# Attention and routed experts on one core: probabilities times values of a head pair in one block per pair where there were two

## The chip, the cores and the metric

The kernel runs on one NeuronCore of one Trainium2 chip. The metric is the device time of one execution in microseconds (us). Lower is better.

## The reference

Causal attention with a bias from running sums, over 8 batches, 8 heads, 576 positions and a head size of 64, in fp32. Its output, reshaped to 4608 tokens of 512 features, goes through a layer of eight experts of which each token uses one.

```python
scores = scale * np.matmul(q, k.transpose(0, 1, 3, 2))
cum = np.cumsum(np.maximum(s, 0.0), axis=-1)
bias = -(cum[:, :, :, None] - cum[:, :, None, :])
scores = np.where(causal, -1000000000.0, scores + np.minimum(bias, 0.0))
attn = np.exp(scores - np.max(scores, axis=-1, keepdims=True))
attn = attn / (np.sum(attn, axis=-1, keepdims=True) + 1e-09)
x = np.matmul(attn, v)                    # -> (4608, 512)
logits = x @ w_gate + modality_bias[modality_id]
e_idx = np.argmax(logits, axis=1)         # one expert for each token
out[mask] = gate_w[mask, None] * (np.maximum(x[mask] @ w1[e], 0.0) @ w2[e])
```

## The kernel before

The first stage is attention. It goes through 32 pairs: a pair is one head of two batches, called `ab` = 0 and 1. The queries of a pair are cut into nine tiles: tiles 0 to 3 are the four blocks of 128 queries of `ab` = 0, tiles 4 to 7 those of `ab` = 1, and tile 8 holds the last 64 queries of both. Tile c (or 4 + c) sees 128 (c + 1) keys because of the mask. `ORDER` takes them as 3, 7, 2, 6, 8, 1, 5, 0, 4.

For each tile there are two steps.

- `score`: TensorE multiplies queries by keys (lines 373 and 395, for tile 8 lines 408 and 409) into a PSUM buffer `sp`, of which there are four (`SPB`). VectorE adds the mask and finds the row's bound (line 397, for tile 8 line 411), and ScalarE takes the exponential and the row's sum (line 417, a column of `sums`).
- `trans`, which I call the turn of a tile: TensorE transposes the exponentials, 128 keys at a time (line 427; line 440 for tile 8), into a PSUM buffer `pt`, of which there are two, and ScalarE copies them into `PT` (line 430; for tile 8 VectorE does, line 446). In a row, the number of transposes or the width tells the tile: four of them (512 columns) are tile 3 or 7, three tile 2 or 6, two tile 1 or 5, one tile 0 or 4. So a copy of 128 columns on line 430 is that of tile 0 or of tile 4.

The turn of a tile is written down three tiles behind its score (`LAG`), so the turns of a pair reach into the scores of the next one. There are three `PT` tiles, and a pair uses two of them.

`tail` is the last step of a pair: the turned probabilities times the values (line 467). The result has the head's 64 features on 64 partitions, and the two batches of a pair stand on partitions 0 to 63 and 64 to 127 of one PSUM tile `o`; each of these matmuls uses one half of TensorE's columns. Keys are summed over five blocks j of 128. Before the change there are two such blocks of matmuls for each pair. Block `g` = 1 covers queries 256 to 575. It is written down after the turn of tile 8, and has ten matmuls. Block `g` = 0 covers queries 0 to 255. It is written down after the turn of tile 4, the last one, and has four. An fp32 matmul shows as two records in the trace, two passes over its columns, so the blocks are 20 and 8 records there.

After a block ScalarE copies 256 columns of `o` into `oT` (line 470), VectorE copies the last 64 queries (line 474), ScalarE adds a small number to the sums (`rs`, line 479), VectorE inverts them (line 480), TensorE multiplies `oT` by a unit matrix with the gate's weights beside it (`pw_`, line 347) into the PSUM tile `ox`, and VectorE scales that by `rs` into `x` (lines 489 and 491).

GpSimd prepares the next pair's queries and keys (lines 323 and 327). The core's order on each engine is made by the scheduler of the framework from the order of the program text and from explicit "issue after" edges; each engine then works through its own list in order.

The second stage is the experts. Its first instruction on TensorE is line 1032 (`tp`), and then lines 1082 and 1057 follow.

Of the kernel before, what the change touches and what calls it, by code (L numbers as in the profile page):

```python
# [7 lines left out]
F32 = mybir.dt.float32  # L8
# [3 lines left out]
AF = mybir.ActivationFunctionType  # L12
ALU = mybir.AluOpType
# [4 lines left out]
P = 128  # L18
KW = 576
XW = 72  # L20

PTS, PTW = 448, 1984
NEG = -8.0e9
EXT = 76
ORDER = (3, 7, 2, 6, 8, 1, 5, 0, 4)
LAG = 3
TD = 1
SPB = 4
# [9 lines left out]
class Attn:  # L38
# [406 lines left out]
                        w = PT[ab][:kp, PTW - 64:].unsqueeze(1)  # L445
                    cp(w, pt[:kp, :P * nj].rearrange("p (j a q) -> p a j q", a=2, q=64)[:, ab])  # L446

    def tail(self, st, g):

        nc = self.nc  # L450
        V, PT, x, h = st["V"], st["PT"], st["x"], st["h"]
        for _ in range(TD):
            yield
        q0, q1 = (256, KW) if g else (0, 256)
        o = st["o"] if g else self.ps2.tile([P, 512], F32, name="o")
        oT = self.oT[st["pi"] % 2]

        pe, self.pe = self.pe, []
        nj = 5 if g else 2
        for j in range(nj):  # L460
            f = max(P * j, q0)
            for ab in range(2):
                r = slice(64 * ab, 64 * ab + 64)
                with ExitStack() as after:
                    for i in pe:
                        after.enter_context(self.tc.issue_after(i))
                    m = nc.tensor.matmul(o[r, f - q0:q1 - q0], V[:, ab, j, :], PT[ab][:, PTS * j + f if j < 4 else PTW - 64:PTS * j + q1 if j < 4 else PTW], start=j == 0, stop=j == nj - 1)  # L467
            pe = [m.ins]
        self.wall = m.ins
        nc.scalar.copy(oT[:, q0:q0 + 256], o[:, :256])  # L470
        if g:
            for ab in range(2):
                r = slice(64 * ab, 64 * ab + 64)
                nc.vector.tensor_copy(oT[r, 512 + 64 * ab:576 + 64 * ab], o[r, 256:320])
        yield
        n = 5 if g else 4
        rs = self.sm.tile([P, 5], F32, name="rs")
        with self.tc.issue_after(self.hold[0]), self.tc.issue_after(self.act):
            nc.scalar.activation(rs[:, :n], st["sums"][:, 4 * g:4 * g + n], AF.Identity, bias=self.eps[:, :1])
            nc.vector.reciprocal(rs[:, :n], rs[:, :n])  # L480
        xo = self.xo
        for u in range(2):
            c = 2 * g + u
            self.pw_(xo[:, 2 * XW * u:2 * XW * u + 2 * XW], oT[:, P * c:P * c + P], self.pw[:, h, :], start=True, stop=True)
        if g:
            self.pw_(xo[:, 4 * XW:5 * XW], oT[:, 512:], self.pq[:, h, :], start=True, stop=True)
        src = xo[:, :4 * XW].rearrange("p (t d) -> p t d", t=4)
        rv = rs[:, :4].unsqueeze(2).broadcast_to([P, 4, XW])
        nc.vector.tensor_tensor(x[g][:, :, :, h], src.rearrange("p t (d r) -> p t d r", r=2), rv.rearrange("p t (d r) -> p t d r", r=2), ALU.mult)
        if g:  # L490
            nc.vector.tensor_scalar(x[2][:, 0, :, h], xo[:, 4 * XW:5 * XW].rearrange("p (d r) -> p d r", r=2), rs[:, 4:5], None, ALU.mult)
        yield

    def run(self, npair, newx, done, setup):

        bg = self.bg = []
        seq = [(pi, i) for pi in range(npair) for i in ORDER]
        sts = {}
        prev, prepg, n = [], None, len(seq)
        for k in range(n + LAG + 9):  # L500
            if k < n:
                pi, i = seq[k]
                if k % 9 == 0:
                    sts[pi] = self.start(pi, newx(pi // 8) if pi % 8 == 0 else sts[pi - 1]["x"])
                    prepg = self.prep(pi + 1) if pi + 1 < npair else None
                with self.behind() if pi or not self.pe else self.tc.issue_after(self.pe[-1]):
                    self.score(sts[pi], i)
                if k in setup:
                    with self.newest():
                        more = setup[k]()  # L510
                        if more is not None:
                            bg.append([more, False])
                if k % 9 == 2 and 0 < pi < npair - 1:
                    self.V[pi + 1] = self.load_v(pi + 1)
                if k % 9 == 7 and 0 < pi < npair - 2:
                    self.raw[pi + 2] = self.load_qk(pi + 2)
                if prepg is not None:
                    next(prepg, 0)
            if prev and next(prev[0][0], 0) == 0:
                _, st, g = prev.pop(0)  # L520
                if g == 0 and st["pi"] % 8 == 7:
                    bg.append([done(st["pi"] // 8, st["x"]), False])
            for j in () if k == LAG else (0, 1) if k == LAG + 1 else (k - LAG,) if LAG < k < n + LAG else ():
                p0, i0 = seq[j]
                with self.behind():
                    self.trans(sts[p0], i0)
                if i0 in (8, ORDER[-1]):
                    g = int(i0 == 8)
                    prev.append((self.tail(sts[p0], g), sts[p0], g))
            if not prev and k >= n + LAG:  # L530
                break
            for b in list(bg):
                if k >= b[1] if b[1] > 1 else k % 9 in QUIET or not b[1]:
                    with self.newest():
                        b[1] = next(b[0], None)
                    if b[1] is None:
                        bg.remove(b)
        assert not prev
        return bg
# [847 lines left out]
```

## Time and profile before

| | |
|---|---|
| median of three runs | 836.78 us (836.66 to 837.16) |
| the profiled execution, its own time | 836.83 us |
| its span, first to last instruction | 835.1 us |
| mean granted TensorE clock | 0.995 |
| busy share of the span: PE, DVE, ACT, POOL | 98%, 65%, 65%, 43% |
| line 467 runs, from its first to its last start | 22.9 to 384.8 us |
| the experts' first matmul on TensorE (line 1032) | 386.17 us |

PE is TensorE's matmuls, PEld its weight loads, DVE is VectorE, ACT is ScalarE, POOL is GpSimd and SP the queue that issues transfers. "Busy" is the time that an engine spent on instructions. Matmuls are pipelined, so the record of a matmul is longer than the distance to the next one, and it is the distance from start to start that tells what it costs.

### The profile page before, as it was taken

To read this page: it belongs to the slowest core of one execution; us is meant where nothing else is said; L and a number is where in the kernel's file an instruction comes from. 1 tells how busy PE (TensorE), PEld (TensorE's weight loads), DVE (VectorE), ACT (ScalarE), POOL (GpSimd) and SP (SyncE) were. 2 spreads that over 40 slices of the span, in tenths; PEclk is the share of its full clock that TensorE was granted. 3 is DMA by queue.
4 is the path that set the end of the run, shared out by engine and by line. 5 is a ranking of instruction groups with operands and counts; after the bars stand their busy time and mean duration, and the time that the engine had idled before them with its cause. 6 is when DMAs were issued, how large, how long until landed. Compare 5 with 4: busy or idle time off the path is not lost. (4 is left out here: it accounts for less than half of the span.)

```text
span 835.1 us, 16829 instructions
## 1 busy us (share of the span) xinstructions
PE 818.3 (98%) x5692; PEld 715.2 (86%) x5692; DVE 545.9 (65%) x1502; ACT 542.1 (65%) x1292; POOL 359.9 (43%) x384
## 2 busy tenths in 40 slices
PE   7999999999999999999999999999999999999996
PEld 7888888888888888887888999998888999988884
DVE  7666667667666677666579865556666655655874
ACT  6788888888888888786365554444555554444763
POOL 8959768887698867993500100000000000000010
PEclk9999999999999999999999999999999999999998
DMA  7665556676557656547498776555556666555960
GB/s 235 180 198 180 178 190 196 213 230 190 167 178 222 196 177 193 175 164 279 173 397 316 297 273 246 205 207 199 214 207 252 255 256 225 216 207 209 376 231 29
DMA packets 68549, 182.31 MB, mean 218 GB/s; under 512 B 7993, under 2 KB 8889, under 8 KB 68334
## 3 DMA queue, kind: packets, MB, share of 16 engines
q1 hardware_dynamic: 62622, 161.17, 57.0%
q0 software_dynamic: 5840, 20.06, 6.2%
q8 instruction: 45, 0.74, 0.4%
q14 instruction: 42, 0.34, 0.1%
HBM read 144.73 MB, written 26.80 MB: 205 GB/s over the span
## 5 line engine op out<-in xcount | busy, mean ns | idle before, releaser
L1068 POOL DMA_INDIRECT out<-ys,oi x36 | 36.5, 1015 | 368.4 <-ACT ys L1067 299.9
L397 DVE CUSTOM_DVE_ANT_0 pe<-sp,mk 128x512 f32<-128x512 f32 (+3 forms) x256 | 120.7, 488 | 57.7 <-PE sp L395 55.2
L417 ACT ACTIVATE pe<-pe,mx 128x512 f32<-128x512 f32 (+3 forms) x256 | 144.5, 565 | 15.6 <-DVE mx L397 10.2
L430 ACT COPY PT<-pt 128x512 f32<-128x512 f32 (+3 forms) x256 | 106.7, 417 | 31.0 <-PE pt L427 27.8
L427 PE MATMUL pt<-ident,pe 128*128 128x128 f32 x640 | 119.2, 284 | 0.7 <-ACT PT L430 0.2
L467 PE MATMUL o<-PT,V 128*64 128x320 f32 (+4 forms) x896 | 108.8, 364 | 2.7 <-DVE PT L446 2.6
L467 PEld LDWEIGHTS o<-PT,V 128*64 128x64 f32 x896 | 75.1, 136 | 36.2 <-DVE PT L446 8.8
L1084 ACT ACTIVATE hT<-hp 128x512 fp32r<-128x512 f32 x72 | 42.8, 595 | 93.1 <-PE hp L1082 92.6
L373 PE MATMUL sp<-KA,QH 128*128 128x256 f32 (+2 forms) x256 | 100.2, 398 | 2.5 <-POOL KA L236 1.8
L427 PEld LDWEIGHTS pt<-ident,pe 128*128 128x128 f32 x640 | 76.2, 144 | 16.1 <-ACT PT L430 6.1
L1082 PE MATMUL hp<-xT,wcb 128*128 128x256 f32 x648 | 89.6, 282 | 0.0
L1082 PE MATMUL hp<-xT,wca 128*128 128x256 f32 x624 | 87.3, 282 | 0.5 <-ACT xT L1034 0.5
L327 POOL TENSOR_TENSOR KA<-rawk,KA 64x576 fp32r<-64x576 f32 x62 | 87.3, 1426 | 0.2
L395 PE MATMUL sp<-KB,QL 76*128 76x256 f32 (+2 forms) x256 | 86.1, 338 | 1.0 <-DMA QL<-ek 1.0
L327 POOL TENSOR_TENSOR QL<-rawq,QH 64x576 fp32r<-64x576 f32 x62 | 86.6, 1413 | 0.2
L1085 DVE SCALAR_TENSOR_TENSOR hT<-hp,hT 128x512 fp32r<-128x512 f32 x72 | 49.5, 688 | 54.7 <-ACT hT L1084 54.5
L1082 PEld LDWEIGHTS hp<-xT,wcb 128*128 128x128 f32 x648 | 83.1, 188 | 0.6
L1082 PEld LDWEIGHTS hp<-xT,wca 128*128 128x128 f32 x624 | 80.4, 188 | 1.4 <-issue 0.7
L1057 PE MATMUL y<-wcb,hT 128*128 128x512 f32 x336 | 81.2, 398 | 0.0
L1057 PEld LDWEIGHTS y<-wcb,hT 128*128 128x128 f32 x336 | 62.8, 188 | 14.7
L323 POOL TENSOR_SCALAR KA<-rawk 128x576 fp32r<-128x576 f32 x60 | 39.4, 670 | 60.2 <-PE sp L373 43.8
L1082 PE MATMUL hp<-xT,wcc 128*128 128x256 f32 x456 | 64.6, 281 | 0.0
(285 smaller groups left out, 1638.4 us busy)
## 6 DMA issues: line engine op xcount, KB each, us to landing
wrbw<-in_w SPq DMA_DIRECT2D x104, 512.0 KB
wraw<-in_w SPq DMA_DIRECT2D x56, 512.0 KB
rawq<-in_qkv SPq DMA_DIRECT2D x31, 576.0 KB
rawk<-in_qkv SPq DMA_DIRECT2D x31, 576.0 KB
xg<-lists SPq DMA_DIRECT2D x18, 576.0 KB
V<-in_qkv SPq DMA_DIRECT2D x32, 320.0 KB
KB<-KA SPq DMA_DIRECT2D x62, 144.0 KB
lists<-z SPq DMA_DIRECT2D x8, 576.0 KB
```

What stands on the lines that cost most here:

```text
L327: self.last = nc.gpsimd.tensor_tensor(o, i, h, ALU.subtract).ins
L373: self.pe.append(self.nc.tensor.matmul(sp[:, :nn], QH[:, q0:q0 + P], self.KA[u][:, ab, :nn], start=True, stop=False).ins)
L395: self.pe.append(nc.tensor.matmul(sp[:, :nn], QL[:EXT, q0:q0 + P], KB[:EXT, ab, :nn], start=False, stop=True).ins)
L397: ins = nc.vector.tensor_tensor_reduce(out=t[:, :n], in0=sp[:, :n], in1=self.mk[:, 512 - n:512], scale=-0.125, scalar=3.0e38, op0=ALU.add, ...
L417: self.act = nc.scalar.activation(t[:, :n], t[:, :n], AF.Exp, bias=m, scale=-1.0, accum_out=st["sums"][:, o:o + 1]).ins
L427: self.pe.append(nc.tensor.transpose(out=pt[:, P * j:P * j + P], in_=pe[:, P * j:P * j + P], identity=self.ident).ins)
L430: cp(w[:, :, v:v + P], pt[:, :P * (c + 1)].rearrange("p (j q) -> p j q", q=P))
L467: m = nc.tensor.matmul(o[r, f - q0:q1 - q0], V[:, ab, j, :], PT[ab][:, PTS * j + f if j < 4 else PTW - 64:PTS * j + q1 if j < 4 else PTW], ...
L1057: self.last[0] = nc.tensor.matmul(y[u], hT[:, a, f, P * u:P * u + P], W[4 + f // 2][:, c, 512 * (f % 2):512 * (f % 2) + 512], start=f == 0 ...
L1082: nc.tensor.matmul(hp[:, u], W[k][:, a, f:f + P], xT[:, c, k], start=k == 0 and i == 0, stop=k == 3 and i == 2)
L1084: hi = nc.scalar.activation(hs, hp, AF.Relu)
L1085: lo = nc.vector.scalar_tensor_tensor(hT[:, 1, 2 * m:2 * m + 2], hp, 0.0, hs.bitcast(F32), ALU.max, ALU.subtract)
```

## The change

The two blocks of a pair become one, which is written down after the turn of tile 4, the pair's last. For each block of keys j, the queries from 128 j to 511 go to `o`, as matmuls of 512, 384, 256 and 128 columns. The last 64 queries go to a second PSUM tile, taken from the ring of `sp`, as five matmuls of 64 columns. That makes 18 matmuls (36 records in the trace) where there were 14 (28 records), over the same number of columns: 1600 for each batch. `oT` is copied by one ScalarE instruction of 512 columns, the sums are handled by one instruction on nine columns on each of the two engines, and the products with `pw` and the scaling follow as before, first for the queries from 256 on, one step later for the others.

```diff
-    def tail(self, st, g):
+    def tail(self, st):
...
-        q0, q1 = (256, KW) if g else (0, 256)
-        o = st["o"] if g else self.ps2.tile([P, 512], F32, name="o")
+        o, ox = st["o"], self.ps1.tile([P, 512], F32, name="sp", bufs=SPB)
...
-        nj = 5 if g else 2
-        for j in range(nj):
-            f = max(P * j, q0)
...
-                    m = nc.tensor.matmul(o[r, f - q0:q1 - q0], V[:, ab, j, :], PT[ab][:, PTS * j + f if j < 4 else PTW - 64:PTS * j + q1 if j < 4 else PTW], start=j == 0, stop=j == nj - 1)
+        for j in range(5):
+            for q0, q1, t, b in ((P * j, 512, o, 0), (512, KW, ox, 512)):
+                if q0 == q1:
+                    continue
...
+                        m = nc.tensor.matmul(t[r, q0 - b:q1 - b], V[:, ab, j, :], PT[ab][:, PTS * j + q0 if j < 4 else PTW - 64:PTS * j + q1 if j < 4 else PTW], start=j == 0, stop=j == (4 if b else 3))
...
-        nc.scalar.copy(oT[:, q0:q0 + 256], o[:, :256])
+        nc.scalar.copy(oT[:, :512], o)
...
-        n = 5 if g else 4
-        rs = self.sm.tile([P, 5], F32, name="rs")
+        rs = self.sm.tile([P, 9], F32, name="rs")
...
-            nc.scalar.activation(rs[:, :n], st["sums"][:, 4 * g:4 * g + n], AF.Identity, bias=self.eps[:, :1])
-            nc.vector.reciprocal(rs[:, :n], rs[:, :n])
+            nc.scalar.activation(rs, st["sums"], AF.Identity, bias=self.eps[:, :1])
+            nc.vector.reciprocal(rs, rs)
...
-                if i0 in (8, ORDER[-1]):
-                    g = int(i0 == 8)
-                    prev.append((self.tail(sts[p0], g), sts[p0], g))
+                if i0 == ORDER[-1]:
+                    prev.append((self.tail(sts[p0]), sts[p0]))
```

Since the scheduler sets the order, more moves than the diff shows. The first place is TensorE in the middle of the attention stage. Before, the block of ten stands between the turns of tile 1 and of tile 5 (each two transposes):

```order
L427 MATMUL pt<-ident,pe 128x128 x2
L467 MATMUL o<-PT_111,V 64x320
L467 MATMUL o<-PT_109,V 64x320
L467 MATMUL o<-PT_111,V 64x320
L467 MATMUL o<-PT_109,V 64x320
L467 MATMUL o<-PT_111,V 64x320
L467 MATMUL o<-PT_109,V 64x320
L467 MATMUL o<-PT_111,V 64x192
L467 MATMUL o<-PT_109,V 64x192
L467 MATMUL o<-PT_111,V 64x64
L467 MATMUL o<-PT_109,V 64x64
L427 MATMUL pt<-ident,pe 128x128 x2
```

Now the only block stands where the block of four was, behind the scores of the next pair's tile 8 (lines 408 and 409) and ahead of the turn of its tile 7:

```order
L427 MATMUL pt<-ident,pe 128x128 x4
L408 MATMUL sp<-KA_105,QH_101 128x288
L409 MATMUL sp<-KB_107,QL_103 128x288
L467 MATMUL o<-PT_111,V 64x512
L467 MATMUL o<-PT_109,V 64x512
L467 MATMUL sp<-PT_111,V 64x64
L467 MATMUL sp<-PT_109,V 64x64
L467 MATMUL o<-PT_111,V 64x384
L467 MATMUL o<-PT_109,V 64x384
L467 MATMUL sp<-PT_111,V 64x64
L467 MATMUL sp<-PT_109,V 64x64
L467 MATMUL o<-PT_111,V 64x256
```

Nothing of line 467 is left between the turns of tiles 1 and 5, and the narrow matmuls into `sp` alternate with the wide ones into `o`.

The second place is ScalarE, from the exponential of tile 4 (`pe`, 128x128) to the copy of `oT` behind the last block. Before, one pair reads:

```order
L417 ACTIVATE pe,sums<-pe,mx 128x128
L417 ACTIVATE pe,sums<-pe,mx 128x512
L470 COPY oT_112<-o 128x256
L430 COPY PT_111<-pt 128x2x128
L430 COPY PT_110<-pt 128x128
L417 ACTIVATE pe,sums<-pe,mx 128x512
L479 ACTIVATE rs<-sums,eps 128x5
L417 ACTIVATE pe,sums<-pe,mx 128x384
L430 COPY PT_111<-pt 128x128
L417 ACTIVATE pe,sums<-pe,mx 128x384
L430 COPY PT_109<-pt 128x4x128
L470 COPY oT_112<-o 128x256
```

Now the copies of the turned tiles 1, 5 and 0 come first, then the exponential of tile 4, and the copy of the turned tile 4 (the second `128x128`) stands behind three exponentials of the next pair (tiles 3, 7 and 2):

```order
L430 COPY PT_109<-pt 128x2x128
L430 COPY PT_110<-pt 128x2x128
L430 COPY PT_109<-pt 128x128
L417 ACTIVATE pe,sums<-pe,mx 128x128
L417 ACTIVATE pe,sums<-pe,mx 128x512 x2
L417 ACTIVATE pe,sums<-pe,mx 128x384
L430 COPY PT_110<-pt 128x128
L417 ACTIVATE pe,sums<-pe,mx 128x384
L430 COPY PT_111<-pt 128x4x128
L417 ACTIVATE pep,sums<-pep,mx 128x576
L470 COPY oT_113<-o 128x512
```

Of the 30 places between two blocks, 17 read like this one (I call them kind A). In 7 the copy of tile 4 stands behind one exponential of the next pair (kind B), as here:

```order
L430 COPY PT_109<-pt 128x128
L417 ACTIVATE pe,sums<-pe,mx 128x128
L417 ACTIVATE pe,sums<-pe,mx 128x512
L430 COPY PT_110<-pt 128x128
L417 ACTIVATE pe,sums<-pe,mx 128x512
```

In the other 6 (kind C) it stands ahead of all of them. The kinds differ in how early the copy of tile 4, the last input of the block, comes. The experts' instructions on TensorE keep their order.

More of the change, by code (lines that the diff above doesn't have):

```diff
@@ L453, in tail @@
             yield
-        q0, q1 = (256, KW) if g else (0, 256)
-        o = st["o"] if g else self.ps2.tile([P, 512], F32, name="o")
+        o, ox = st["o"], self.ps1.tile([P, 512], F32, name="sp", bufs=SPB)
         oT = self.oT[st["pi"] % 2]
         pe, self.pe = self.pe, []
-        nj = 5 if g else 2
-        for j in range(nj):
-            f = max(P * j, q0)
[L462 to L468, printed above, removed]
@@ L469, in tail @@
-        self.wall = m.ins
[L470 to L474, printed above, removed]
+        for j in range(5):
+            for q0, q1, t, b in ((P * j, 512, o, 0), (512, KW, ox, 512)):
+                if q0 == q1:
+                    continue
+                for ab in range(2):
+                    r = slice(64 * ab, 64 * ab + 64)
+                    with ExitStack() as after:
+                        for i in pe:
+                            after.enter_context(self.tc.issue_after(i))
+                        m = nc.tensor.matmul(t[r, q0 - b:q1 - b], V[:, ab, j, :], PT[ab][:, PTS * j + q0 if j < 4 else PTW - 64:PTS * j + q1 if j < 4 else PTW], start=j == 0, stop=j == (4 if b else 3))
+                pe = [m.ins]
@@ L475, in tail @@
+        self.wall = m.ins
+        nc.scalar.copy(oT[:, :512], o)
+        for ab in range(2):
+            r = slice(64 * ab, 64 * ab + 64)
+            nc.vector.tensor_copy(oT[r, 512 + 64 * ab:576 + 64 * ab], ox[r, :64])
         yield
-        n = 5 if g else 4
-        rs = self.sm.tile([P, 5], F32, name="rs")
+        rs = self.sm.tile([P, 9], F32, name="rs")
         with self.tc.issue_after(self.hold[0]), self.tc.issue_after(self.act):
-            nc.scalar.activation(rs[:, :n], st["sums"][:, 4 * g:4 * g + n], AF.Identity, bias=self.eps[:, :1])
-            nc.vector.reciprocal(rs[:, :n], rs[:, :n])
+            nc.scalar.activation(rs, st["sums"], AF.Identity, bias=self.eps[:, :1])
+            nc.vector.reciprocal(rs, rs)
@@ L481, in tail @@
         xo = self.xo
[L482 to L489, printed above, removed]
@@ L490, in tail @@
-        if g:
-            nc.vector.tensor_scalar(x[2][:, 0, :, h], xo[:, 4 * XW:5 * XW].rearrange("p (d r) -> p d r", r=2), rs[:, 4:5], None, ALU.mult)
-        yield
+        for g in (1, 0):
+            for u in range(2):
+                c = 2 * g + u
+                self.pw_(xo[:, 2 * XW * u:2 * XW * u + 2 * XW], oT[:, P * c:P * c + P], self.pw[:, h, :], start=True, stop=True)
+            if g:
+                self.pw_(xo[:, 4 * XW:5 * XW], oT[:, 512:], self.pq[:, h, :], start=True, stop=True)
+            src = xo[:, :4 * XW].rearrange("p (t d) -> p t d", t=4)
+            rv = rs[:, 4 * g:4 * g + 4].unsqueeze(2).broadcast_to([P, 4, XW])
+            nc.vector.tensor_tensor(x[g][:, :, :, h], src.rearrange("p t (d r) -> p t d r", r=2), rv.rearrange("p t (d r) -> p t d r", r=2), ALU.mult)
+            if g:
+                nc.vector.tensor_scalar(x[2][:, 0, :, h], xo[:, 4 * XW:5 * XW].rearrange("p (d r) -> p d r", r=2), rs[:, 8:9], None, ALU.mult)
+            yield
@@ L519, in run @@
             if prev and next(prev[0][0], 0) == 0:
-                _, st, g = prev.pop(0)
-                if g == 0 and st["pi"] % 8 == 7:
+                _, st = prev.pop(0)
+                if st["pi"] % 8 == 7:
                     bg.append([done(st["pi"] // 8, st["x"]), False])
```

## The prediction

> **What bounds the kernel now.** I read the busy times by stretches first, then one pair of the attention stage on TensorE and on ScalarE in order of time. The stretch 120 to 180 us lies in the middle of attention (its columns: busy us and instructions of PE, PEld, DVE, ACT, POOL, then granted clock, DMA share, GB/s):
>
> ```profile
> 120.00:180.00 60.00, 59.98 (x469) 51.26 (x469) 40.81 (x180) 50.33 (x165) 49.37 (x49) 1.00 0.66 209
> ```
>
> TensorE shows no idle time, ScalarE and GpSimd are at 0.83, VectorE at 0.68. But records of matmuls overlap and are longer than their pitch, so this is no proof that TensorE never waits. One pair, TensorE, by start:
>
> ```profile
> 150.22 2.60 PE L467 MATMUL o<-PT,V 128*64 128x320 f32 x20
> 152.75 0.44 PE L427 MATMUL pt<-ident,pe 128*128 128x128 f32 x2
> 153.49 0.65 PE L347 MATMUL ox<-pw,oT 128*128 128x144 f32 x4
> 153.98 0.34 PE L347 MATMUL ox<-pq,oT 128*128 128x72 f32 x2
> 154.15 0.27 PE L427 MATMUL pt<-ident,pe 128*128 128x128 f32 x1
> ...
> 154.62 0.27 PE L427 MATMUL pt<-ident,pe 128*128 128x128 f32 x1
> ...
> 155.08 0.60 PE L427 MATMUL pt<-ident,pe 128*128 128x128 f32 x4
> 155.44 0.38 PE L408 MATMUL sp<-KA,QH 128*128 128x288 f32 x1
> ...
> 156.46 0.29 PE L409 MATMUL sp<-KB,QL 76*128 76x288 f32 x1
> 156.68 0.87 PE L467 MATMUL o<-PT,V 128*64 128x256 f32 x8
> 157.49 0.66 PE L427 MATMUL pt<-ident,pe 128*128 128x128 f32 x4
> ...
> 158.22 0.66 PE L347 MATMUL ox<-pw,oT 128*128 128x144 f32 x4
> 158.71 0.49 PE L427 MATMUL pt<-ident,pe 128*128 128x128 f32 x3
> ...
> 159.28 0.54 PE L427 MATMUL pt<-ident,pe 128*128 128x128 f32 x3
> ...
> 159.89 0.27 PE L440 MATMUL o<-ident,pep 128*64 128x128 f32 x1
> ...
> 161.60 0.81 PE L467 MATMUL o<-PT,V 128*64 128x320 f32 x3
> ```
>
> From block to block a pair takes 161.60 − 150.22 = 11.38 us. And ScalarE in the same pair:
>
> ```profile
> 154.46 0.27 ACT L430 COPY PT<-pt 128x128 f32<-128x128 f32 x1 [0.87 <-PE pt L427]
> 154.62 0.73 ACT L417 ACTIVATE pe<-pe,mx 128x512 f32<-128x512 f32 x1
> ...
> 155.34 0.29 ACT L479 ACTIVATE rs<-sums,eps 128x5 f32<-128x5 f32 x1
> 155.53 0.61 ACT L417 ACTIVATE pe<-pe,mx 128x384 f32<-128x384 f32 x1
> ...
> 156.13 0.25 ACT L430 COPY PT<-pt 128x128 f32<-128x128 f32 x1
> 156.28 0.62 ACT L417 ACTIVATE pe<-pe,mx 128x384 f32<-128x384 f32 x1
> ...
> 157.60 0.37 ACT L470 COPY oT<-o 128x256 f32<-128x256 f32 x1
> 157.87 0.78 ACT L417 ACTIVATE pep<-pep,mx 128x576 f32<-128x576 f32 x1
> ...
> 158.64 0.57 ACT L430 COPY PT<-pt 128x512 f32<-128x512 f32 x1
> 159.10 0.52 ACT L417 ACTIVATE pe<-pe,mx 128x256 f32<-128x256 f32 x1
> ...
> 161.02 0.41 ACT L417 ACTIVATE pe<-pe,mx 128x128 f32<-128x128 f32 x1
> ```
>
> Behind the second block ScalarE runs without a gap, from 157.60 on. While the block of 20 runs it gets nothing to turn, hence the 0.87 idle at 154.46. So the pair is a ring: TensorE bounds it in one part, the chain through ScalarE in another. Its waits on TensorE show at the last pair, where nothing else is in flight:
>
> ```profile
> 379.35 0.44 PE L427 MATMUL pt<-ident,pe 128*128 128x128 f32 x2 [0.21 <-ACT PT L430]
> 380.11 2.28 PE L467 MATMUL o<-PT,V 128*64 128x320 f32 x20 [0.32 <-DVE PT L446]
> ```
>
> The block of 20 waits for VectorE's copies of tile 8; over the run that comes to
>
> ```profile
>   DVE PT L446: 11.4, 34
> ```
>
> which is 11.4 us in 34 waits.
>
> **The cost of the matmuls.** A block of 20 that found all its inputs ready, and the mean records by width:
>
> ```profile
> 207.62 2.28 PE L467 MATMUL o<-PT,V 128*64 128x320 f32 x20 [0.43 <-DVE PT L446]
> 209.82 0.44 PE L427 MATMUL pt<-ident,pe 128*128 128x128 f32 x2
> ...
> L467 PE MATMUL o<-PT,V 128*64 128x192 f32 x4 | 0.8, 326 | 0.0
> L467 PE MATMUL o<-PT,V 128*64 128x64 f32 x4 | 0.6, 220 | 0.0
> L467 PE MATMUL o<-PT,V 128*64 128x128 f32 x4 | 0.4, 272 | 0.0
> ```
>
> For each batch the block of 20 streams 2 passes of 1216 columns in 2.20 us, the block of 8 (156.68 to 157.49) 2 passes of 384 in 0.81. The difference is 1.39 us for 1664 columns, 0.835 ns a column; then 0.81 − 768 × 0.000835 leaves 0.17 us for entering and leaving a block. The merged block streams 3200 columns: 2.67 + 0.17 = 2.84 us. Before, a pair spends 2.53 (150.22 to 152.75, its second batch held back by VectorE) and 0.81: 3.34. So the block itself saves 0.50 us a pair, and the wait for VectorE ahead of it goes as well, as tile 8 is turned long before.
>
> Each batch now has 18 passes instead of 14, ten of them of 64 columns where there were two. The narrow ones are in that sum at 0.053 us each. Records of 64, 128 and 192 columns differ by 52 and 54 ns, so width alone counts; a fixed cost for each pass would have to come out of the 0.17 that 4 passes and 10 passes leave alike, so I take none. The Trainium skill ("TensorEngine Tiling (Array Packing)", Instruction Overhead) gives each matmul about 60 cycles of overhead; if that is added to every pass, and a cycle is taken as one column's 0.835 ns, an estimate from that page is 0.05 us for each of the 4 added passes, 0.2 us a pair, and 839.6 for the whole. The rows above, where blocks of 4 and of 10 passes leave the same rest, speak against it; without it the sum stays as below.
>
> The other edits: ScalarE copies once 512 instead of twice 256 columns (pitch 0.46, as for `PT` at 158.64, against 2 × 0.27 at 157.60) and adds to the sums once instead of twice (saving 0.19, the pitch at 155.34). VectorE loses one inversion. Both lie where these engines have slack, at nothing; the single copy of 0.57 comes 0.2 us later than one of 0.37, and the four transposes and the scores ahead of the products (157.49 to 158.22, 0.73) just cover 0.10 + 0.57 + 0.05. The narrow result takes one of four `sp` buffers until VectorE has copied it, right behind the block; the score that needs that buffer next comes four allocations later, more than 2 us. GpSimd's work and the transfers keep their order against a pair of nearly equal length: nothing.
>
> **One pair, placed row behind row.** I set 0 at the first transpose behind the block. Up to the turn of tile 0 TensorE does: turn of 7 and score of 1 (0.73), products (153.49 to 154.15, 0.66), turn of 2 and score of 5 (158.71 to 159.28, 0.57), turn of 6 and score of 0 (0.61), a wait for ScalarE's copy of tile 2 to free `pt` (0.2, as at 379.35), turn of 8 and score of 4 (0.73 + 0.06), turn of 1, score of 3 and products (152.75 to 153.49, 0.74 less 0.06, and 158.22 to 158.71, 0.49), turn of 5 and score of 7 (0.68). Sum 5.41. From there the block can start by two ways:
>
> - TensorE: turn of 0 and one score (154.15 to 154.62, 0.47), the other score 0.36, turn of 4 0.11 after a wait of 0.1 for its exponential, tile 8's scores 1.15 (155.44 to 156.46 and one more), turn of 3 0.36, and 0.09 of switching: 2.64.
> - ScalarE, kind A: 0.31 from the turn of 0 to its copy (154.15 to 154.46), copy 0.16, exponential of 4 0.40, of 3 and 7 0.72 each, of 2 0.60, copy of 4 0.25, release 0.05: 3.21.
>
> In kind A ScalarE's chain comes last: 5.41 + 3.21 + 2.84 = 11.46; kind B, where the copy of 4 is out of the way, 5.41 + 2.64 + 2.84 = 10.89. In kind C the exponential of 3 waits for that copy and the turn of 3 waits for the exponential: 0.31 + 0.16 + 0.40 to the turn of 4's release, 0.1 + 0.37 to its copy, 0.15, exponential 0.72, turn of 3 0.5, scores 0.29 and switching 0.09, 3.09 in all, so 11.34. My pieces carry some exposed starts twice (0.06 at each first transpose behind a wait), so I take 0.05 off each: 11.41, 10.84 and 11.29 against 11.38.
>
> The sum: 17 pairs of A at +0.03, 7 of B at −0.54, 6 of C at −0.09 give +0.5 − 3.8 − 0.5 = −3.8 us. At the end of attention nothing hides the last pair. Before:
>
> ```profile
> 378.29 0.28 PE L395 MATMUL sp<-KB,QL 76*128 76x256 f32 x1
> ...
> 383.83 1.29 PE L467 MATMUL o<-PT,V 128*64 128x256 f32 x8
> 385.58 0.76 PE L347 MATMUL ox<-pw,oT 128*128 128x144 f32 x4 [0.46 <-ACT oT L470]
> 386.17 1.04 PE L1032 MATMUL tp<-ident,xg 128*128 128x128 f32 x8
> ```
>
> that is 7.88 from the last score to the experts. After: about 3.1 to the copy of tile 4, 2.84 for the block, 0.72 for its copy, products 0.66, VectorE's scaling of the first half 0.3, products 0.5: 8.1 to 8.4. I add 0.4. The expert stage has the same order and TensorE's whole time, so it moves as a piece. In all −3.4 us from the profiled execution's 836.83 (span 835.1 and 1.7 around it), which stands 0.05 above the median: 833.4.
>
> **Rivals.**
> 1. TensorE alone bounds (much faster). If the chain through ScalarE is shorter than placed, by 0.57 or more in A and 0.45 in C, all 30 pairs take 10.84: −16.2, and with +0.4 about 821. For it: ScalarE before shows gaps such as 0.87. Against: it has these gaps because its inputs come late, and A keeps three exponentials ahead of the copy the block needs.
> 2. No change, 837: the copy of tile 4 comes last in B too, for example because VectorE's masking of tile 3 is late; then −3.8 is lost and 837 stands. For it: VectorE gets its two scaling passes and four copies closer together than before. Against: its share is 0.68.
> 3. Slower: the narrow passes hold the array. The two passes of 72 columns at 153.98 take 0.17 until the next start at 154.15, where 144 columns at 0.835 ns make 0.12: 0.025 too much a pass, perhaps 0.05 if it falls on one. Eight more such passes cost 0.2 to 0.4 a pair, in all kinds, 6 to 12 us over 31 pairs: 840 to 846. It decides from 0.014 a pass on, where 3.4 us are eaten up. Against: those two are followed by a load for 128 columns, here loads are for 64. The rule of the Trainium skill above, added to each pass, would give this rival's lower end.
>
> That the change doesn't do what it says is excluded by the order: one block a pair stands there.
>
> **Numbers.** Forecast (the sum within its errors, 0.1 us a pair, so 830 to 836.5) 0.50; rival 1, or a part of it, 0.16; rival 2 0.16; rival 3, or a chain longer by 0.1 us and more, 0.18. A measurement of this kernel tells about 0.2%, 1.7 us, from no change. Faster by more (below 835.1): 0.16 and most of the forecast's, together 0.60. Within: 0.20. Slower: 0.20. The range goes from most of rival 1, 822, to most of rival 3, 845; the forecast's own is 830 to 836.5.
>
> **What would show it.** In the changed profile: the block starts to next transposes in 2.84 us where its second batch isn't held back (rival 3: 3.0 to 3.3); in kind A the second batch's first matmul waits for "ACT PT L430", about 0.5 us behind the first batch's, and the pair takes 11.3 to 11.5; in B 10.8 to 10.9, in C 11.2 to 11.3; no wait for "DVE PT L446" ahead of line 467; ScalarE is idle about 1.2 us ahead of the copy of `oT`. Wrong would be: waits of TensorE at a place that I pass at nothing (line 347 for `oT`, line 395 for GpSimd's or a transfer's data), or all kinds alike.

## The result and the profile after

| | median us | runs | ratio to before, 95% interval |
|---|---|---|---|
| before | 836.37 (835.78 to 837.16) | 8 | |
| after | 839.42 (839.03 to 840.8) | 8 | 1.004 [1.0029, 1.0051] |

The change made the kernel 3 us slower, where 3.4 us less had been forecast. The profiled execution of after took 839.37 us, its span is 837.6, 2.5 more than before's.

The stretch 120 to 180 us of after, with the columns of the prediction's row:

```profile
120.00:180.00 60.00, 59.87 (x510) 48.66 (x511) 38.33 (x175) 49.27 (x155) 48.31 (x47) 1.00 0.65 207
```

Weight loads, VectorE and ScalarE have less to do, by 2.6, 2.5 and 1.1 us, and yet the stage isn't shorter (it ends at 388.57 us where it ended at 386.17, see below). So less work was put into a ring that takes as long. A plain pair of kind A on TensorE, by start:

```profile
192.87 0.66 PE L427 MATMUL pt<-ident,pe 128*128 128x128 f32 x4
...
198.31 0.27 PE L427 MATMUL pt<-ident,pe 128*128 128x128 f32 x1
...
199.33 0.33 PE L427 MATMUL pt<-ident,pe 128*128 128x128 f32 x1
...
201.11 1.45 PE L467 MATMUL o<-PT,V 128*64 128x512 f32 x4
...
204.37 0.66 PE L427 MATMUL pt<-ident,pe 128*128 128x128 f32 x4
```

The pair takes 204.37 − 192.87 = 11.50 us. The turn of tile 0 stands at 198.31, 5.44 us into the pair, the turn of tile 4 at 199.33, and the block starts at 201.11. ScalarE in the same pair:

```profile
198.62 0.27 ACT L430 COPY PT<-pt 128x128 f32<-128x128 f32 x1 [0.20 <-PE pt L427]
198.78 0.40 ACT L417 ACTIVATE pe<-pe,mx 128x128 f32<-128x128 f32 x1
...
199.18 0.71 ACT L417 ACTIVATE pe<-pe,mx 128x512 f32<-128x512 f32 x1
...
199.88 0.71 ACT L417 ACTIVATE pe<-pe,mx 128x512 f32<-128x512 f32 x1
...
200.59 0.60 ACT L417 ACTIVATE pe<-pe,mx 128x384 f32<-128x384 f32 x1
...
201.19 0.25 ACT L430 COPY PT<-pt 128x128 f32<-128x128 f32 x1
...
204.24 0.59 ACT L470 COPY oT<-o 128x512 f32<-128x512 f32 x1 [0.96 <-PE o L467]
```

The copy of tile 4 ends at 201.44, 0.33 us after the block has started. The second batch of the block needs it, and with 0.05 for the release it starts at about 201.49, 3.18 us behind the turn of tile 0. From there the block takes 2.88. In the list of waits (total us, times, longest) this is the row

```profile
PEld o L467 <- ACT PT L430: 4.4, 18, 0.5
```

These are 18 waits, for the 17 pairs of kind A and the last pair. No wait for "DVE PT L446" is left ahead of the block.

In kind C the copy isn't late, so its block shows what 36 records cost when all inputs are there. One such pair, next to the routing (the choice of an expert for each token of a group; VectorE's line 669 belongs to it), all engines:

```profile
117.84 0.42 DVE L669 TENSOR_REDUCE ox<-x 128x32 f32<-128x256 f32 x1
...
118.17 0.28 DVE L397 CUSTOM_DVE_ANT_0 pe<-sp,mk 128x128 f32<-128x128 f32 x1
...
119.09 0.33 PE L427 MATMUL pt<-ident,pe 128*128 128x128 f32 x1
...
119.46 0.27 ACT L430 COPY PT<-pt 128x128 f32<-128x128 f32 x1 [0.42 <-PE pt L427]
...
119.62 0.73 ACT L417 ACTIVATE pe<-pe,mx 128x512 f32<-128x512 f32 x1
...
120.49 0.66 PE L427 MATMUL pt<-ident,pe 128*128 128x128 f32 x4
...
121.47 1.08 PE L467 MATMUL o<-PT,V 128*64 128x512 f32 x4
...
124.36 0.33 PE L427 MATMUL pt<-ident,pe 128*128 128x128 f32 x1
```

124.36 − 121.47 = 2.89 us for the block. Ahead of it stands a chain of seven steps with little slack: the reduction holds VectorE, so the mask of tile 4 starts at 118.17; then come its exponential, its turn (119.09), its copy, the exponential of tile 3, the turn of tile 3 (120.49), and the block.

And the end of attention on TensorE:

```profile
379.62 0.28 PE L395 MATMUL sp<-KB,QL 76*128 76x256 f32 x1
...
382.22 0.33 PE L427 MATMUL pt<-ident,pe 128*128 128x128 f32 x1 [1.08 <-ACT pe L417]
382.48 1.50 PE L467 MATMUL o<-PT,V 128*64 128x512 f32 x4
...
386.30 0.76 PE L347 MATMUL ox<-pw,oT 128*128 128x144 f32 x4 [0.45 <-ACT oT L470]
...
387.98 0.76 PE L347 MATMUL ox<-pw,oT 128*128 128x144 f32 x4 [0.75 <-DVE xq L490]
388.57 1.04 PE L1030 MATMUL tp<-ident,xg 128*128 128x128 f32 x8
```

The experts start at 388.57, where before they started at 386.17.

The 2.4 us between these two starts can be split up. I take the ends of the blocks in both traces (in before, the end of the block of 8 of the same pair) and list after minus before, in us:

| part | predicted | measured |
|---|---|---|
| end of the first block (the start-up) | 0 | −0.29 |
| 17 pairs of kind A | +0.5 | +1.93 |
| 7 pairs of kind B | −3.8 | −3.55 |
| 6 pairs of kind C | −0.5 | +2.44 |
| behind the 31st block, to the experts' first matmul | +0.4 | +1.87 |
| sum | −3.4 | +2.40 |

Within kind A twelve plain pairs take 11.50 (+0.11 each), three next to routing 11.9 (+0.56 each), and two that were 0.7 to 0.9 us longer than others in before's profiled execution are 1.0 us shorter together, for reasons that I don't know. Within kind C three pairs next to routing lose 0.22 each, one gains 0.30, and pairs 2 and 3 take 12.41 and 12.45 where before they took 11.40 and 11.39: 2.1 us in two pairs.

### The profile page after: what moved, and what is told of

Read it like the earlier page. It is cut to its first block, busy times and chain, and to the rows that moved or that the text cites. A ratio compares the mean times of both kernels' runs of the same rounds, so it can differ in the third digit from the quotient of the medians.

```text
span 837.6 us, 17313 instructions
## 1 busy us (share of the span) xinstructions
PE 819.4 (98%) x5948; PEld 703.9 (84%) x5948; DVE 529.4 (63%) x1470; ACT 533.6 (64%) x1228; POOL 361.1 (43%) x384
## 5 line engine op out<-in xcount | busy, mean ns | idle before, releaser
L417 ACT ACTIVATE pe<-pe,mx 128x512 f32<-128x512 f32 (+3 forms) x256 | 142.4, 559 | 13.8 <-DVE mx L397 13.0
L397 DVE CUSTOM_DVE_ANT_0 pe<-sp,mk 128x512 f32<-128x512 f32 (+3 forms) x256 | 116.8, 481 | 47.5 <-PE sp L395 40.6
L430 ACT COPY PT<-pt 128x512 f32<-128x512 f32 (+3 forms) x256 | 103.9, 419 | 40.9 <-PE pt L427 39.2
L427 PE MATMUL pt<-ident,pe 128*128 128x128 f32 x640 | 115.4, 278 | 3.5 <-ACT pe L417 1.8
L467 PE MATMUL o<-PT,V 128*64 128x256 f32 (+3 forms) x512 | 94.9, 440 | 0.0
L467 PEld LDWEIGHTS sp<-PT,V 128*64 128x64 f32 x640 | 47.8, 137 | 28.0 <-issue 15.1
```

The lines of the kernel that those rows point to most:

```text
L397: ins = nc.vector.tensor_tensor_reduce(out=t[:, :n], in0=sp[:, :n], in1=self.mk[:, 512 - n:512], scale=-0.125, scalar=3.0e38, op0=ALU.add, ...
L417: self.act = nc.scalar.activation(t[:, :n], t[:, :n], AF.Exp, bias=m, scale=-1.0, accum_out=st["sums"][:, o:o + 1]).ins
L427: self.pe.append(nc.tensor.transpose(out=pt[:, P * j:P * j + P], in_=pe[:, P * j:P * j + P], identity=self.ident).ins)
L430: cp(w[:, :, v:v + P], pt[:, :P * (c + 1)].rearrange("p (j q) -> p j q", q=P))
L467: m = nc.tensor.matmul(t[r, q0 - b:q1 - b], V[:, ab, j, :], PT[ab][:, PTS * j + q0 if j < 4 else PTW - 64:PTS * j + q1 if j < 4 else PTW], ...
```

## The experiments

Theory 1: the merged block needs every copy of the pair, so in kind A ScalarE's chain to the copy of tile 4 sets the pair, and the last pair has no work to put beside it. Theory 2: one long block in which TensorE feeds nobody starves the other engines wherever the copy stands. Theory 3 (the prediction's third rival): narrow passes hold the array; the block of 2.89 already speaks against it.

**The copy of tile 4 early.** After, with a higher priority for the turn of tile 4, which moves it and its copy up in the scheduler's order:

```diff
-                with self.behind():
+                with self.behind(), (self.tc.high_priority(offset=20) if i0 == 4 else ExitStack()):
                     self.trans(sts[p0], i0)
```

> The changed kernel, with ScalarE's copy of the turned tile 4 one place earlier in 17 pairs: behind one exponential of the next pair and no longer behind three (kind A becomes kind B; nothing is added or left out). Theory 1, ScalarE's chain up to that copy sets the pair in kind A: those pairs fall from 11.50 us to about 10.85, the three of them with routing work beside them from 11.90 to about 11.3, so the kernel from 839.4 to about 829.5. Rival, the single long block starves ScalarE and VectorE wherever the copy stands, and the short kind B pairs are pairs that catch up after the long ones with routing work: pairs stay at 11.4 to 11.5 and the time at 838 to 839.5.

Measured: 832.24 us (831.97 to 833.19), 0.9944 [0.9931, 0.9957] of before. Theory 2 falls: one edit of an order takes 7 us off. But a steady pair, one away from routing and stores, takes 11.12, not 10.85, and the time is 2.7 above the 829.5 that was expected. Such a pair on TensorE, by start:

```profile
168.21 0.66 PE L427 MATMUL pt<-ident,pe 128*128 128x128 f32 x4
...
173.65 0.27 PE L427 MATMUL pt<-ident,pe 128*128 128x128 f32 x1
...
174.67 0.33 PE L427 MATMUL pt<-ident,pe 128*128 128x128 f32 x1
...
176.45 1.08 PE L467 MATMUL o<-PT,V 128*64 128x512 f32 x4
...
179.33 0.66 PE L427 MATMUL pt<-ident,pe 128*128 128x128 f32 x4
```

and on ScalarE:

```profile
173.96 0.27 ACT L430 COPY PT<-pt 128x128 f32<-128x128 f32 x1 [0.21 <-PE pt L427]
174.12 0.41 ACT L417 ACTIVATE pe<-pe,mx 128x128 f32<-128x128 f32 x1
...
174.52 0.71 ACT L417 ACTIVATE pe<-pe,mx 128x512 f32<-128x512 f32 x1
...
175.22 0.25 ACT L430 COPY PT<-pt 128x128 f32<-128x128 f32 x1
```

The copy ends at 175.47, a microsecond ahead of the block. What is late now is one step earlier: the turn of tile 4 (174.67) waits 0.36 us for its exponential, and that stands behind the copy of tile 0 (173.96).

**The last pair in two blocks again.** After, with the old code of the two blocks kept for one pair:

```diff
-                if i0 == ORDER[-1]:
+                if p0 == npair - 1:
+                    if i0 in (8, ORDER[-1]):
+                        prev.append((self.tail2(sts[p0], int(i0 == 8)), dict(pi=0) if i0 == 8 else sts[p0]))
+                elif i0 == ORDER[-1]:
                     prev.append((self.tail(sts[p0]), sts[p0]))
```

> The changed kernel, with the two old blocks for the last pair alone. Theory 1, the last pair has no scores to hide the single block and what follows it, and costs about 1.9 us more than before: the experts' first matmul starts 1.5 to 2 us earlier than in the changed kernel (388.57), the kernel takes about 837.7. Rival, the end of attention is hidden by other work, and the change loses its time in the pairs alone: 839.4, no change.

Measured: 838.8 (837.86 to 840.63), 1.0024 [1.0015, 1.0033]. That is 0.6 less than after, where 1.7 had been expected, and the intervals of the two ratios overlap; what follows is read from the trace. From the end of the 31st block to the experts it takes 11.30 us, against 12.39 in after and 10.52 in before. So 1.1 of the 1.87 lies behind the last score, in the one block and what follows it. TensorE there:

```profile
382.16 2.27 PE L512 MATMUL o<-PT,V 128*64 128x320 f32 x20 [0.80 <-DVE PT L446]
...
385.88 1.29 PE L512 MATMUL o<-PT,V 128*64 128x256 f32 x8
387.63 0.76 PE L347 MATMUL ox<-pw,oT 128*128 128x144 f32 x4 [0.46 <-ACT oT L515]
388.22 1.04 PE L1079 MATMUL tp<-ident,xg 128*128 128x128 f32 x8
```

The block of 20 waits 0.80 for VectorE, where it waited 0.32 before. The other 0.8 us stay: from the end of the 31st block to the last score it takes 3.44 in both (after: 376.18 to 379.62), 2.64 before. The traces show what was added there: four transposes of tile 8 (378.90 in after) stand ahead of the last score, where in before they start behind it (378.48), and so do two products of 72 columns. Taking these out again wasn't tried.

**Both.** After, with the two edits together.

> The changed kernel with both edits: the early copy of the turned tile 4 and the two old blocks for the last pair. Theory 1: both gains add up, about 828, under the kernel before (836.4) by 1%. Rival of a block that starves the other engines: 837.5 to 839.5.

Measured: 830.94 (830.63 to 832.15), 0.9932 [0.9918, 0.9945]. The two edits add up (the second takes 1.3 us off the first experiment's time), and 3 us are missing from the 828, mostly for the reason of the first experiment.

**The copy of tile 4 on VectorE.** After, with `PTDVE = (4, 8)` for `PTDVE = (8,)`; these are the tiles that VectorE copies out of `pt`.

> The changed kernel, with the copy of the turned tile 4 on VectorE in place of ScalarE. Theory 1: the block no longer waits for ScalarE's chain; the pairs of kind A fall to 10.9 to 11.2, limited by the place of the copy in VectorE's list, the time to 830 to 835. Rival, the block's length alone: 839.

Measured: 832.56 (831.66 to 833.26), 0.9947 [0.9933, 0.996], with steady pairs of 11.12. Off ScalarE altogether, the copy is worth as much as early on ScalarE: beyond that point it no longer counts.

**The control: before, with the early copy.**

> The kernel before, with the same edit as in the first experiment: the turn of tile 4 gets a higher priority, so that ScalarE's copy of it stands right behind that of tile 0, ahead of the exponentials of tiles 3, 7 and 2. Theory 1 (only the merged block waits for that copy; before, the copy ended 0.3 us ahead of the block of 8): no change, 836.0 to 837.2. Rival (an early copy of tile 4 is worth 0.3 us a pair whatever the blocks are, so the first experiment says nothing of the change): 828 to 832.

Measured: 835.97 (835.21 to 836.96) against 836.27, 0.9991 [0.9982, 1.0001]. No change that can be told, though in the trace the copy of tile 4 does stand right behind that of tile 0: an early copy is worth something to the merged block alone.

**The turn of tile 0 early as well.** The version "both", with `i0 in (0, 4)` for `i0 == 4`.

> The third experiment (early copy of tile 4, last pair in two blocks), and the turn of tile 0 gets the higher priority as well, so that it stands ahead of the copy of tile 5. Theory (a steady pair takes 11.12 instead of 10.83 because the exponential of tile 4 waits behind the copy of tile 0, and with it the turn of tile 4): the copy of tile 0 is 0.3 to 0.4 us earlier, a steady pair takes 10.85 to 10.9, and with 12 to 17 such pairs the time is 826.5 to 828. Rival (something else sets the turn of tile 4, such as the score of tile 4 and VectorE's mask): 11.1 a pair, 830.9.

Measured: 826.06 (825.23 to 826.77), 0.9868 [0.9849, 0.9887]: the fastest of all versions, 1.3% ahead of before. A steady pair, TensorE and then ScalarE:

```profile
165.73 0.66 PE L427 MATMUL pt<-ident,pe 128*128 128x128 f32 x4
...
170.36 0.49 PE L427 MATMUL pt<-ident,pe 128*128 128x128 f32 x3
...
171.87 0.27 PE L427 MATMUL pt<-ident,pe 128*128 128x128 f32 x1
...
173.58 1.08 PE L467 MATMUL o<-PT,V 128*64 128x512 f32 x4
...
176.47 0.65 PE L427 MATMUL pt<-ident,pe 128*128 128x128 f32 x4
```

```profile
170.78 0.54 ACT L430 COPY PT<-pt 128x128 f32<-128x128 f32 x2 [0.81 <-PE pt L427]
171.21 0.41 ACT L417 ACTIVATE pe<-pe,mx 128x128 f32<-128x128 f32 x1
```

The turn of tile 0 now follows that of tile 5 directly (three transposes at 170.36), and the exponential of tile 4 starts 5.48 us into the pair, where it was 174.12 − 168.21 = 5.91. The pair takes 10.74, a little less than the 10.85 to 10.9 that were expected.

**Pairs 2 and 3.** In after TensorE's order there differs: the second matmuls (line 395) of tiles 3, 7, 2 and 6 stand behind the turn of tile 4. In before those of tiles 3, 7 and 2 stand ahead of it (46.17, 49.43 and 50.63 against 50.81). Pair 2 on TensorE in before:

```profile
46.17 0.47 PE L395 MATMUL sp<-KB,QL 76*128 76x512 f32 x1
...
49.43 0.40 PE L395 MATMUL sp<-KB,QL 76*128 76x512 f32 x1
...
50.81 0.27 PE L427 MATMUL pt<-ident,pe 128*128 128x128 f32 x1
```

and in after, all engines:

```profile
47.91 0.33 PE L427 MATMUL pt<-ident,pe 128*128 128x128 f32 x1
...
48.01 1.04 PE L395 MATMUL sp<-KB,QL 76*128 76x512 f32 x4
...
48.52 0.69 DVE L397 CUSTOM_DVE_ANT_0 pe<-sp,mk 128x512 f32<-128x512 f32 x1 [1.25 <-PE sp L395]
...
49.31 0.72 ACT L417 ACTIVATE pe<-pe,mx 128x512 f32<-128x512 f32 x1 [0.77 <-DVE mx L397]
...
50.18 0.66 PE L427 MATMUL pt<-ident,pe 128*128 128x128 f32 x4
```

VectorE waits 1.25 us for the scores of tile 3, ScalarE 0.77 for VectorE, and the turn of tile 3 comes late. From the turn of tile 4 to the block (51.30) it takes 3.39 us, in the plain pair above 1.78. No wait for a transfer shows on any engine in either pair (41.8 to 66.7 us). These two pairs are those in which the running sums are stored (`save`, ten transfers on SP, in before as well), so the stores were written down elsewhere:

```diff
-... 17: lambda: A.save(0), 26: lambda: A.save(1), ...
+... 53: lambda: A.save(0), 62: lambda: A.save(1), ...
```

> The changed kernel, in which the two steps that store the running sums (ten transfers on SP) are written down four pairs later, so that they fall into pairs 6 and 7 instead of 2 and 3. With them the written order of TensorE moves: the second matmuls (line 395) of tiles 3, 7, 2 and 6 stand behind the turn of tile 4 in those pairs. Theory A (this order is what makes pairs 2 and 3 take 12.4 us where others take 11.5): pairs 2 and 3 take 11.5, pairs 6 and 7 take 12.4, and the total stays at 839.4, within 0.6. Rival (the transfers of the first pairs are late, whatever the order): pairs 2 and 3 stay at 12.4 and pairs 6 and 7 too take longer than 11.5, 839.4 to 841.5.

Measured: 840.86 (839.96 to 842.77), 1.0046 [1.0029, 1.0063], 1.4 above after, where theory A had 0.6 at most and the rival up to 2.1. Pairs 2 and 3 take 11.49 and 11.50, as theory A has it. Of the new pairs, 7 takes 12.55, close to its 12.4, with line 395 behind the turn of tile 4 again (109.43 behind 109.33), and 6 takes 14.12. But within pair 6 TensorE's granted clock was halved for 3.4 us (0.50 in this row, with the columns of the first one above):

```profile
97.67:101.07 3.40, 3.40 (x13) 2.16 (x14) 1.40 (x6) 2.94 (x9) 3.40 (x3) 0.50 0.45 102
```

If half of this stretch was lost, an estimate, pair 6 would have taken 12.4 as well; the profiled execution took 842.77, 1.9 above the median. So the place of the stores makes the long pairs, and theory A has their length. Where the 1.4 us of the median come from stays open. The next run is the version with tiles 0 and 4 early, with the stores at 48 and 57.

> The run before this one, with the two steps that store the running sums at another place of pairs 5 and 6, where the written order of TensorE puts the second matmuls of tiles 3, 7, 2 and 6 behind the turn of tile 4 in one pair instead of two. Theory A (each such pair costs 1.0 us): 0.7 to 1.3 us less than the run before this one. Rival (late transfers): no difference.

Measured: 827.91 (827.44 to 828.7), 0.9894 [0.9875, 0.9913], 1.85 us slower than without that edit, where 0.7 to 1.3 less had been expected. Pairs 2 and 3 take 10.74 and 10.75 instead of 12.30 and 12.45, pairs 6 and 7 13.11 and 13.40 instead of 10.74 and 10.76. There all the scores of tiles 3, 7, 2 and 6, first and second matmuls (lines 373 and 395), stand behind the turn of tile 4, and not in one pair but in both (90.34 in pair 6). Pair 7 on TensorE:

```profile
103.45 0.33 PE L427 MATMUL pt<-ident,pe 128*128 128x128 f32 x1 [1.08 <-ACT pe L417]
...
104.30 0.40 PE L395 MATMUL sp<-KB,QL 76*128 76x512 f32 x1
```

And the preparation by GpSimd is late:

```profile
95.83 1.30 POOL L323 TENSOR_SCALAR KA<-rawk 128x576 fp32r<-128x576 f32 x2 [5.79 <-DMA rawk<-in_qkv]
```

It waits 5.79 us for a load that SP issues behind the stores, and is done with the keys (line 327) at 103.90; TensorE waits 0.3 us for them. In pair 3 of after it was done at 57.25, for scores that start at 58.38. So in pairs 2 and 3 of after the trace shows the order alone, and in pairs 6 and 7 here the order and a late load, which no run took apart. Why the scheduler orders the scores in this way beside the stores stays open.

## Why the prediction was wrong

**Right.** The block: 2.89 us measured, 2.84 predicted. Rival 3 had 3.0 to 3.3 and is refuted: eight more narrow passes cost at most 0.05. One of my arguments for it was circular: that blocks of 4 and of 10 passes leave the same 0.17 follows from fitting the 0.835 ns a column to these two blocks. What decides is the merged block, in which a pass of 64 columns takes 0.057 us on average from start to start, 0.004 more than its columns. The Trainium skill's overhead of some 60 cycles for each matmul ("TensorEngine Tiling (Array Packing)", Instruction Overhead), added to every pass, would make an estimated 3.04; the measurement decides against adding it here. That its time of 839.6 for the whole lies near the measured 839.4 is chance. Also right: the mechanism of kind A (second batch held back, 3.18 from the turn of tile 0 where 3.21 was predicted), the end of the waits for "DVE PT L446", and, by luck as told below, the sum over kind B.

**The step that failed most: kind C, −0.5 against +2.44.** I took it as one steady kind, placed by the rows of an undisturbed pair. But kind C is just where the stream is disturbed: its pairs stand beside the stores (2 and 3) and beside the routing. Pairs 2 and 3 alone make 2.1 of the 2.94 that I was off. For them I had written that GpSimd's work and the transfers "keep their order against a pair of nearly equal length: nothing". The transfers do keep their order, and no wait for one shows; what I had wrong is that after the change, too, the pairs beside them would be like the others. Before, with the same stores, these two pairs were as short as any (11.40 and 11.39). With the block of 20 gone from the middle, the scheduler puts the second matmuls of four scores behind the turn of tile 4, and everything behind them is late. Beside the routing I gave the mask of tile 4 no competitor on VectorE; the trace has a reduction of 0.42 ahead of it, at the head of the chain of seven steps. That routing pairs lose by that chain is read from the trace and was not tried.

**The tail, +0.4 against +1.87.** From the last score to the experts it takes 388.57 − 379.62 = 8.95, where I had 8.1 to 8.4: the second products start 387.98 − 386.30 = 1.68 behind the first, where I had 0.66 + 0.3 = 0.96, because VectorE scales the first half in two instructions and TensorE waits 0.75 for the second of them. The rest, 0.8, lies ahead of the last score, where I had no term and where tile 8's transposes and two products had moved.

**Kind A, +0.5 against +1.93.** A plain pair is 5.44 + 3.18 + 2.88 = 11.50. Each piece is within 0.04 of its own, and the rest is the 0.05 that I took off for doubly counted starts: there was nothing to take off. So +0.03 became +0.11. For the three pairs next to routing I had no term of their own: there ScalarE's copy of tile 4 starts 0.39 behind the block (133.09 against 132.70) where it starts 0.08 behind it in a plain pair, which makes most of the +0.56.

**Kind B was right for a wrong reason.** The seven are no steady pairs: three of 11.30 stand beside routing, where before took 11.65, and the others, of 10.8 to 11.0, right behind such pairs, where TensorE's order differs. In a steady stream, shown by the first experiment, kind B takes 5.44 + 2.80 + 2.88 = 11.12: my way over TensorE was 0.16 short (2.64 against 2.80), because the turn of tile 4 waits longer for its exponential. Rival 1's pair of 10.84 exists (10.74), but only with two turns moved.

So the change does what it says on TensorE, at the price that was worked out. Its gain went into new waits. One, which the prediction had, is that of the merged block for the latest of all copies, 0.38 us in each plain pair of kind A by the first experiment. The others, which it had not, are the late scores beside the stores and the end of attention. With that copy and the one ahead of it early, and the last pair in two blocks, the kernel takes 826.06.

## What to carry to other kernels

When pieces of work are merged, the merged piece waits for the latest of all inputs; place that input in the order of the engine that makes it first, and price the merge by the pair that results, not by the matmuls saved. A small priority edit on that input, tried on the kernel before as a control, tells in one run whether it is the input or the merge. Rows of a quiet stretch don't speak for pairs beside other work (stores, reductions): group these apart, and compare each engine's order there before and after the change.

## What was not expected of the hardware

The two batches of a block, each on its half of TensorE's columns, don't wait for each other: in kind A the first batch starts at 201.11 and streams while the second stands until about 201.49. The start-up differs between profiled executions of nearly equal code: the first block ended between 29.3 and 31.6 us in the ten profiles, a spread of 2.2 us where the change makes 3. So sums over pairs were compared from that block's end on. Part of it goes with the clock: in seven of the ten (before among them, 17.43 to 20.83 us) the granted clock is 0.50 for 3.4 us within the first 21 us, and there the block ended at 30.05 to 31.57; in the other three (after among them) it ended at 29.34 to 29.93.
